# A new price list for a kernel's own scheduler: durations, engine occupation and hand-over delays kept apart

## The chip, the cores and the metric

The kernel runs on one core of one Trainium2 chip. Five engines run their own instruction streams and meet only at semaphores: TensorE (PE, matmuls; its weight loads are listed as PEld), VectorE (DVE), ScalarE (ACT), GpSimd (POOL) and SyncE (SP, which issues the DMAs here). The metric is the device time of one execution, in microseconds; lower is better.

## The reference

Two layers, run twice on one sequence of 2048 tokens of width 448, bf16. Cut to what matters:

```python
def _A_ref(x, mem0, Wq, Wk, Wv, Wo, seg_len):     # 64 segments of 32 tokens, 16 heads of 256
    mem = mem0                                     # 8 memory tokens
    for s in range(n_seg):
        h = concat([mem, x[segment s]])            # 40 tokens
        p = softmax(mask(h Wq (h Wk)^T * scale))
        o = (p (h Wv)) Wo
        mem = o[:, :M]                             # the next segment needs this
        outs.append(o[:, M:])

def _B_ref(x, W_gate, W_up, W_down):
    return (relu(x W_gate) * (x W_up)) W_down

x = x + A(layernorm(x)); x = x + B(layernorm(x))
x = x + A(layernorm(x)); x = x + B(layernorm(x))
```

The memory makes each A layer a recurrence of 64 steps: a segment can't start its scores before the segment ahead has given its 8 memory rows.

## The kernel before

Wq and Wk are multiplied into one matrix A per head at the start, Wv and Wo into one matrix B, so that the scores are h A h^T and the output is p h B. All stays in SBUF after that.

*The recurrence* (`chain`, `middle`). One step serves a segment of both A layers at once, the second layer 7 segments behind. PE multiplies the memory rows by A (L750, eight small tiles at a time), ACT or DVE evicts the four banks to `Usb`, DVE transposes blocks of 32 (L858, L866), PE makes the scores (L881), DVE finds the row minimum (L892), ACT takes the exponentials (L894), DVE normalizes (L898, L899), PE transposes (L914), ACT or DVE evicts, PE applies the probabilities to the rows (L938, L942), an eviction to `YTm`, PE multiplies by B (L785, 56 matmuls in three groups), ACT and DVE split the result in a high and a low part (L792, L793), PE turns it into columns and rows of the next memory (L804, L814), an eviction to `mT`, and the next step begins at L750. `ride` lets some masked rows of the second layer go along (L903 to L911).

*The other work* (`tiles`). For each tile of 128 tokens: the attention of its token rows by four groups of heads (`att_group`: L1021, L1046, a softmax on DVE and ACT at L1053 to L1059, L1065, L938, L1093), the layer norm (`norm`: L957 to L972, a scaled copy `xn`, whose rows a DMA carries to `HR`), and the gated layer (`glu_units`, `glu_down`: L1115, L1120, L1121, L1133). Buffers bound how far this work may run ahead: eight PSUM banks, two `Ug`, one `YT`, one `hG`, two `xn`, six `X`.

*The order* comes from the kernel's own planner. Every operation is recorded by `_Sched.add` with its engine or choice of engines (an eviction may go to ACT or DVE), a cost in ns, what it reads and writes, and a priority (recurrence first). `schedule` then plays the program through: it takes the engine that can start next, and on it, of the operations that are ready at that time, recurrence first, then those in PE's present tiling mode, then program order. The result is a fixed order for each engine, and the choice of ACT or DVE and of the PSUM bank. `emit` writes the order with semaphore waits. Nothing is decided at run time, so an engine whose next instruction isn't ready waits, whatever else could run.

In the planner before, an operation holds its engine for its whole cost. A turn of PE's tiling mode adds 100 ns. A result of PE can be used by another engine 260 ns after its end, any other result 100 ns after, on the same engine 40 ns after. A DMA takes SP for 570 ns and lands 2000 ns after its bytes at 240 bytes per ns. Eviction and matmul costs come from `ev_cost`, `dv_cost` and `mm_cost`; some small operations have a number of their own at the call. In the opening steps, when PE has a gap, `filler` puts dummy matmuls into it (L1148).

Of the kernel before, what the change touches and what calls it, by code (L numbers as in the profile page):

```python
# [31 lines left out]
class _Op:  # L32
    __slots__ = ("idx", "engs", "cost", "fn", "deps", "prio", "dma", "eng", "ndep", "users", "ready",
                 "start", "end", "need_inc", "val", "clock", "slot", "seq", "alloc", "mode",
                 "touch")
# [16 lines left out]
class _Sched:  # L52
# [8 lines left out]
    TURN = 100.0  # L61
# [11 lines left out]
    def add(self, engs, cost, fn, r=(), w=(), prio=1, dma=0, alloc=(), room=(), mode=0, now=None):  # L73
# [4 lines left out]
        o.fn = fn  # L78
        o.deps = {}
# [48 lines left out]

    def schedule(self):
# [33 lines left out]
        while left:  # L163
# [28 lines left out]
            c = o.cost[e]  # L192
            if e == "pe" and self.warm and self.warm[1] <= o.prio[0]:
                bank = self.warm[0]
                if o.prio[0] >= self.warm[2]:
                    if held is not None:
                        empty[bank] = held
                    self.warm = None
                elif held is None and o.prio[1] == 0 and empty[bank][0] is not None:
                    held, empty[bank] = empty[bank], (None, ())  # L200
                n = int((t0 - free[e] - 300.0) * self.warm[3] / 190.0) if self.warm and held else 0
                if n > 0:
                    f = self.filler(n, held[1], free[e], len(seq))
                    order[e].append(f)
                    seq.append(f)
                    mode = f.mode
            if e == "pe":
                if mode is not None and o.mode != mode:
                    c += self.TURN
                mode = o.mode  # L210
            o.start = t0
            if o.dma:
                free[e] = t0 + c
                dma_free = max(dma_free, t0) + o.dma / 240.0
                o.end = dma_free + 2000.0
            else:
                free[e] = t0 + c
                o.end = t0 + c
# [4 lines left out]
            for h in o.touch:  # L223
                h.left -= 1
                if not h.left:
                    empty[h.name] = (max(p.end + (0.0 if p.eng == "pe" else 100.0) for p in h.ops), tuple(h.ops))
            for u in o.users:
                u.ndep -= 1
                for x in u.engs:
                    if o.dma:  # L230
                        t = o.end + 100.0
                    elif x == e:
                        t = o.end if (e == "pe" or u.deps[o] is None) else o.end + 40.0
                    elif e == "pe":
                        t = o.end + 260.0
                    else:
                        t = o.end + 100.0
# [9 lines left out]
    def filler(self, n, deps, start, seq):  # L247
# [5 lines left out]
        f.prio, f.start, f.end, f.need_inc, f.seq, f.users, f.alloc = (0, 9), start, start + n * 190.0, False, seq, [], ()  # L253
# [148 lines left out]
class _Kernel:  # L402
# [190 lines left out]
    def dma(self, dst, src, nbytes, r=(), w=(), prio=1):  # L593
        self.s.add("sp", 570, lambda E, e: E.dma_start(dst, src), r=r, w=w, dma=nbytes, prio=prio)  # L594
# [131 lines left out]
    def chain(self, step):  # L726
# [14 lines left out]
        for half in range(2):  # L741
# [11 lines left out]
            s.add("pe", 7 * (D / 2.33 + 3), fn, r=["mTm", "mTr"] + self.A_all, w=ub, alloc=ub, room=[("Usb", 2 * half + v) for v in range(2)], mode=4, **P)  # L753
# [26 lines left out]
        for lo, hi in ((0, 5), (5, 10), (10, 14)):  # L780
# [7 lines left out]
            s.add("pe", (hi - lo) * (D / 2.33 + 3), oo, r=ykeys + self.B_all, w=[bo], alloc=[bo] if lo == 0 else (), mode=1, **P)  # L788
# [3 lines left out]
        s.add("act", 145 + 0.82 * D, lambda E, e: E.activation(hi_[:, mid], bo.ap()[:, 0:D], ACT.Copy), r=[bo], w=["Ohi"], **P)  # L792
# [58 lines left out]
    def turn_u(self, half, P):  # L851
# [4 lines left out]
        for hh in range(2):  # L856
            out = self.uT[:, 0:3, :, 8 * hh + 4 * half:8 * hh + 4 * half + 4, :].rearrange("p k c a t -> p a (k c) t")
            self.s.add("dve", dv_cost(384), lambda E, e, out=out, hh=hh: E.transpose(out, heads[hh]),  # L858
                       r=[("Usb", 2 * half + v) for v in range(2)], w=[f"uT{half}"], **P)

    def turn_tail(self, hh, P):
# [4 lines left out]
        self.s.add("dve", dv_cost(256), lambda E, e: E.transpose(out, src), r=[("Usb", r) for r in range(4)], w=["uT2"], **P)  # L866

    def middle(self, act, m, row, col, P):
# [15 lines left out]
        s.add("pe", 4 * na * 28, sc, r=uk + [q for c, sg, l in act for q in self.ht_keys(l, sg)], w=[bq], alloc=[bq], **P)  # L884
# [6 lines left out]
        if m["mask"] is None:  # L891
            s.add("dve", dv_cost(40 * na), lambda E, e: E.tensor_reduce(mx, S_(), AX.X, ALU.min), r=[bq], w=[k_("mx")], **P)  # L892
            for c, sg, l in act:
                s.add("act", 214, lambda E, e, c=c: E.activation(m["E"][:, c, 0:L], psS()[:, c, 0:L], ACT.Exp, bias=m["st"][:, c:c + 1], scale=-1.0,  # L894
                                                                 accum_out=m["st"][:, 2 + c:3 + c]), r=[bq, k_("mx")], w=[k_(f"E{c}")], **P)
            for c, sg, l in act:
                b = sg % 2
                s.add("dve", 110, lambda E, e, c=c: E.reciprocal(m["st"][:, 4 + c:5 + c], m["st"][:, 2 + c:3 + c]), r=[k_(f"E{c}")], w=[k_(f"rc{c}")], **P)  # L898
                s.add("dve", 134, lambda E, e, c=c, b=b: E.tensor_scalar(Pv[:, b, 0:L], m["E"][:, c, 0:L], m["st"][:, 4 + c:5 + c], None, op0=ALU.mult),  # L899
                      r=[k_(f"E{c}"), k_(f"rc{c}")], w=[k_(f"P{c}")], **P)  # L900
        else:
# [4 lines left out]
            s.add("act", 165 + 33 * na, lambda E, e: E.activation(E_, T_, ACT.Exp, scale=-1.0), r=[k_("Tm")], w=[k_("Em")], **P)  # L906
            s.add("dve", dv_cost(40 * na), lambda E, e: E.tensor_reduce(sm, E_, AX.X, ALU.add), r=[k_("Em")], w=[k_("sm")], **P)
            s.add("dve", 125, lambda E, e: E.reciprocal(rc, sm), r=[k_("sm")], w=[k_("rc")], **P)
            for c, sg, l in act:
                b = sg % 2  # L910
                s.add("dve", 134, lambda E, e, c=c, b=b: E.tensor_scalar(Pv[:, b, 0:L], m["E"][:, c, 0:L], m["st"][:, 4 + c:5 + c], None, op0=ALU.mult),  # L911
# [16 lines left out]
        s.add("pe", 4 * 56, yy, r=[k_("PT")] + [q for c, sg, l in act for q in self.hr_keys(l, sg)], w=yb, alloc=yb, mode=2, **P)  # L928
# [21 lines left out]
    def norm(self, t, dst):  # L950
# [6 lines left out]
        s.add("dve", 566, lambda E, e: E.bn_stats(st[:, 0:6], X[:, :]), r=[xk], w=[("st", i)])  # L957
        s.add("dve", 134, lambda E, e: E.bn_aggr(st[:, 6:8], st[:, 0:6]), r=[("st", i)], w=[("st2", i)])
        s.add("act", 253, lambda E, e: E.activation(st[:, 8:9], st[:, 7:8], ACT.Ln, bias=self.cvec[:, 0:1], scale=1.0),
              r=[("st2", i), "cvec"], w=[("st3", i)])  # L960
        s.add("act", 204, lambda E, e: E.activation(st[:, 9:10], st[:, 8:9], ACT.Exp, scale=-0.5), r=[("st3", i)], w=[("st4", i)])
# [34 lines left out]
    def att_group(self, l, t, g, bo):  # L996
# [52 lines left out]
        s.add("pe", 16 * 28, sc, r=uk + hk, w=[bs], alloc=[bs], room=[k_("Tx")])  # L1049
# [6 lines left out]
        s.add("act", 296, lambda E, e: E.activation(T[:, :, :], T[:, :, :], ACT.Exp, scale=-1.0), w=[k_("Tx")])  # L1056
        s.add("dve", dv_cost(160), lambda E, e: E.tensor_reduce(sm, T[:, :, :], AX.X, ALU.add), r=[k_("Tx")], w=[k_("sm")])
        s.add("dve", 134, lambda E, e: E.reciprocal(rc, sm), r=[k_("sm")], w=[k_("rc")])
# [12 lines left out]
        for p in range(2):  # L1071
# [10 lines left out]
            s.add("pe", 4 * 56 + 4, yy, r=["PTx"] + hk, w=yb, alloc=yb, room=[("YT", yi, p, h) for h in range(2)], mode=2)  # L1082
# [18 lines left out]
    def glu_units(self, t, g, qs, i):  # L1101
        s = self.s
        G, hG = self.G2[g], self.hG[i]
        for q in qs:
# [15 lines left out]
            s.add("act", 145 + 0.82 * N, lambda E, e, dst=dst, z=two[0], N=N: E.activation(dst, z.ap()[:, 0:N], ACT.Relu), r=[two[0]], w=[("hG", i, q)])  # L1120
# [140 lines left out]
```

## Time and profile before

| | |
|---|---|
| median of 3 runs | 1662.86 us (1659.91 to 1664.81) |
| the profiled execution | 1664.92 us |
| its span, first to last instruction | 1662.8 us |
| instructions | 83559 |
| matmuls, and weight loads | 38134 each |
| DVE, ACT instructions | 3378, 2281 |
| granted TensorE clock, mean | 0.994 |
| bytes moved by DMA | 33.03 MB, mean 20 GB/s |

A profile row of the timeline starts with its start and length in us; then engine, line, operation, output and input tiles and their shapes, and in brackets how long the engine stood idle before it and which instruction released it. A row of a group has its total and its mean ns, then the idle time before it. PE rows overlap: a matmul of 128 columns shows 217 ns (L1021) though the next one starts long before it ends. Line numbers are those of the kernel before; in the changed file the same statement stands up to 7 lines further down.

### The profile page before, as it was taken

The numbers are of one execution on the slowest core, as the hardware profiler recorded it, in microseconds if no ns is written. First come the engines' busy times: TensorE is split into PE (matmuls) and PEld (weight loads), VectorE is DVE, ScalarE is ACT, GpSimd is POOL, SyncE is SP. The second block draws the span as 40 slices with busy tenths as digits, with TensorE's granted clock in tenths as the row PEclk, the third lists the DMA queues.
The fourth block names the chain that finished last, engine by engine and source line by source line (L and its number), as shares of the span: only waits on it lengthen the run. The fifth ranks groups of instructions, "written<-read, shape, count | busy, mean of one in ns | idle before, by whom it ended". The sixth has DMA issues, their size and how long they took to land.

```text
span 1662.8 us, 83559 instructions
## 1 busy us (share of the span) xinstructions
PE 1599.4 (96%) x38134; PEld 1123.4 (68%) x38134; DVE 1167.1 (70%) x3378; ACT 842.1 (51%) x2281; POOL 95.3 (6%) x342
## 2 busy tenths in 40 slices
PE   6999898999999999999999999999999999999997
PEld 4646565677676767766766776776867666767775
DVE  6646565777677777777677876786777777777563
ACT  5734344555555555545454554465455546444442
POOL 2000000000000000000000000000000000000000
PEclk9999999999999999999999999999999999999999
DMA  9350000000000000000000000000000000000000
GB/s 229 103 151 15 5 10 7 6 4 7 7 7 4 14 4 15 4 15 4 4 16 12 7 4 14 4 15 4 12 6 13 7 6 13 4 10 4 12 6 7
DMA packets 44976, 33.03 MB, mean 20 GB/s; under 512 B 17984, under 2 KB 43728, under 8 KB 44624
## 3 DMA queue, kind: packets, MB, share of 16 engines
q1 hardware_dynamic: 44624, 27.70, 6.4%
q8 instruction: 299, 4.90, 1.3%
q14 instruction: 53, 0.43, 0.1%
HBM read 21.36 MB, written 1.84 MB: 14 GB/s over the span
## 4 chain that ended last, share of the span: by engine, by line
PE 79%; DVE 11%; issue 4%; ACT 3%; SPq 2%; DMA 1%; POOL 0%; POOLq 0%; DVEq 0%
PE psG L1021 14%; PE psG L1093 12%; PE psC L785 10%; PE psG L1115 8%; PE psC L750 7%; PE psG L1133 3%; PE psG L750 3%; PE psG L632 3%; DVE uT L858 2%; PE psG L938 2%; SPq L594 2%; PE psG L1046 2%; PE psG L785 2%; PE psC L804 1%; PE psC L814 1%
## 5 line engine op out<-in xcount | busy, mean ns | idle before, releaser
L1093 PE MATMUL psG<-Bsb,YT 128*128 128x448 bf16 x1288 | 273.6, 352 | 3.6 <-DVE YT L349 1.8
L1021 PE MATMUL psG<-HT,A 64*128 64x128 bf16 x5196 | 270.2, 217 | 2.3 <-DVE Usb L349 0.8
L1021 PE MATMUL psG<-HX,A 64*128 64x128 bf16 x3897 | 231.6, 217 | 0.1
L346 ACT ACTIVATE Ug<-psG 64x128 bf16<-64x128 f32 (+2 forms) x454 | 159.4, 375 | 101.8 <-PE psG L1021 91.8
L1115 PE MATMUL psG<-G,glu 64*128 64x128 bf16 x6160 | 188.8, 217 | 3.3 <-DVE G L349 2.2
L1021 PEld LDWEIGHTS psG<-HT,A 64*128 64x128 bf16 x5196 | 181.9, 95 | 13.0 <-issue 4.5
L1115 PEld LDWEIGHTS psG<-G,glu 64*128 64x128 bf16 x6160 | 178.0, 95 | 14.2 <-issue 6.9
L785 PE MATMUL psC<-Bsb,YTm 128*32 128x448 bf16 x3360 | 173.1, 358 | 5.9 <-DVE YTm L349 4.0
L1093 PEld LDWEIGHTS psG<-Bsb,YT 128*128 128x128 bf16 x1288 | 115.2, 98 | 93.5 <-DVE YT L349 2.4
L750 PE MATMUL psG<-A,mT 64*32 64x448 bf16 x4088 | 163.3, 350 | 1.7 <-DVE mT L349 0.9
L858 DVE STREAM_TRANSPOSE uT<-Usb 128x384 bf16<-128x384 bf16 x280 | 156.0, 560 | 4.7 <-ACT Usb L346 0.2
L750 PE MATMUL psC<-A,mT 64*32 64x448 bf16 x3752 | 155.1, 350 | 0.8 <-ACT YT L346 0.4
L1021 PEld LDWEIGHTS psG<-HX,A 64*128 64x128 bf16 x3897 | 147.5, 95 | 0.2 <-issue 0.2
L349 DVE CAST Ug<-psG 64x128 bf16<-64x128 f32 (+2 forms) x287 | 118.3, 428 | 38.5 <-PE psG L1021 34.6
L785 PEld LDWEIGHTS psC<-Bsb,YTm 128*32 128x32 bf16 x3360 | 85.4, 98 | 77.5 <-DVE YTm L349 5.4
L1121 DVE TENSOR_TENSOR hG<-hG,psG 128x512 bf16<-128x512 bf16 (+1 forms) x125 | 75.4, 617 | 66.0 <-ACT hG L1120 65.4
L1120 ACT ACTIVATE hG<-psG 128x512 bf16<-128x512 f32 (+1 forms) x127 | 68.9, 542 | 103.9 <-PE psG L1115 100.4
L346 ACT ACTIVATE YT<-psG 128x448 bf16<-128x448 f32 x222 | 110.5, 548 | 20.9 <-PE psG L942 20.1
L750 PEld LDWEIGHTS psC<-A,mT 64*32 64x32 bf16 x3752 | 80.4, 92 | 59.5 <-DVE PTx L349 2.6
L349 DVE CAST Usb<-psG 128x448 bf16<-128x448 f32 x105 | 63.7, 606 | 60.6 <-PE psG L750 60.4
L346 ACT ACTIVATE Usb<-psC 128x448 bf16<-128x448 f32 x105 | 57.1, 544 | 85.9 <-PE psG L750 65.7
L750 PEld LDWEIGHTS psG<-A,mT 64*32 64x32 bf16 x4088 | 84.2, 92 | 22.3 <-DVE HT L349 4.4
(224 smaller groups left out, 2877.3 us busy)
## 6 DMA issues: line engine op xcount, KB each, us to landing
glu<-in_A_Wo_dram SPq DMA_DIRECT2D x8, 448.0 KB
Bsb<-in_A_Wq_dram SPq DMA_DIRECT2D x8, 384.0 KB
Bsb<-in_A_Wk_dram SPq DMA_DIRECT2D x8, 384.0 KB
glu<-in_A_Wv_dram SPq DMA_DIRECT2D x8, 384.0 KB
HR<-xn SPq DMA_DIRECT2D x128, 24.0 KB
HR<-xn SPq DMA_DIRECT2D x128, 4.0 KB
X<-in_A_x_dram SPq DMA_DIRECT2D x16, 112.0 KB
Tsb<-stage SPq DMA_DIRECT2D x112, 7.0 KB
```

Source lines behind the costliest of these rows:

```text
L346: return E.activation(out, i, ACT.Copy, scale=1.0 if scale is None else scale)
L349: return E.tensor_copy(out, i)
L632: i = E.matmul(bk.ap()[row0:row0 + mn, 0:D], lhsT=lhs[:, et, m0:m0 + mn], rhs=rhs[:, et, :], start=(et == 0), stop=(et == 1), tile_positio ...
L750: i = E.matmul(ub[v].ap()[32 * j:32 * j + 32, 0:D], lhsT=self.mT[rw, b, :], rhs=cols, start=(b == 0), stop=(b == 6), tile_position=(64 * v ...
L785: x = E.matmul(bo.ap()[32 * j:32 * j + 32, 0:D], lhsT=self.YTm[:, q, :], rhs=self.Bsb[:, chunks[q], :], start=(i == 0), stop=(i == 13), ti ...
L858: self.s.add("dve", dv_cost(384), lambda E, e, out=out, hh=hh: E.transpose(out, heads[hh]), r=[("Usb", 2 * half + v) for v in range(2)], w ...
L1021: i = E.matmul(ub[v].ap()[:, 128 * n:128 * n + 128], lhsT=self.A[rw, b, a0:a0 + 128], rhs=HT[rw, b, :, 0:SEG] if b < 4 else HX[rw, b - 4, ...
L1093: i = E.matmul(bo.ap()[:, 0:D], lhsT=YT[:, c, :], rhs=self.Bsb[:, 14 * g + c, :], start=(g == 0 and c == 0), stop=(g == 3 and c == 13))
L1115: i_ = E.matmul(two[v].ap()[:, 128 * c:128 * c + 128], lhsT=self.Wgu[rw, b, f0:f0 + 128], rhs=G[rw, b, :], start=(b == 0), stop=(b == 6), ...
L1120: s.add("act", 145 + 0.82 * N, lambda E, e, dst=dst, z=two[0], N=N: E.activation(dst, z.ap()[:, 0:N], ACT.Relu), r=[two[0]], w=[("hG", i, q)])
L1121: s.add("dve", dv_cost(N), lambda E, e, z=two[1], N=N, dst=dst: E.tensor_tensor(dst, dst, z.ap()[:, 0:N], ALU.mult), r=[two[1]], w=[("hG", ...
L1133: i_ = E.matmul(bk.ap()[:, 0:D], lhsT=hG[:, c, :], rhs=self.Wd[:, c, :], start=(c == 0), stop=(c == NFC - 1))
```

## The change

Only the planner and the costs handed to it change. No instruction is added, removed or altered; which engine evicts a bank, which bank is used, the order on each engine and the number of dummy matmuls follow from the planner.

- An operation on ACT, DVE or POOL now has a duration (until its result is there) and a shorter occupation of its engine: duration less `PIPE` (103, 82 and 60 ns), or `busy` where it is given.
- PE is free when the last matmul has been fed in; the result is there 162 ns later (`PE_END`). A turn (94 ns) delays the start.
- A result reaches another engine after that engine's `SEEN` (58 to PE, 38 to ACT and DVE, 62 to POOL, 60 to SP), the same engine after `SELF` (24, 34, 61).
- A DMA takes SP for 700 ns and lands after 1800 ns.
- The formulas and single costs are replaced: evictions, DVE operations and small ACT operations are longer, matmuls a little shorter.

```diff
-    TURN = 100.0
+    TURN = 94.0
+    PIPE = {"act": 103.0, "dve": 82.0, "pool": 60.0}
+    SELF = {"act": 24.0, "dve": 34.0, "pool": 61.0}
+    SEEN = {"pe": 58.0, "act": 38.0, "dve": 38.0, "pool": 62.0, "sp": 60.0}
+    PE_END = 162.0
...
                 if mode is not None and o.mode != mode:
-                    c += self.TURN
+                    turn = self.TURN
...
-                o.end = dma_free + 2000.0
+                o.end = dma_free + 1800.0
+            elif e == "pe":
+                t0 = max(t0, free[e] + turn)
+                o.start = t0
+                free[e] = t0 + c
+                o.end = t0 + c + self.PE_END
             else:
-                free[e] = t0 + c
+                free[e] = t0 + (c - self.PIPE[e] if o.busy is None else o.busy)
                 o.end = t0 + c
...
-                    empty[h.name] = (max(p.end + (0.0 if p.eng == "pe" else 100.0) for p in h.ops), tuple(h.ops))
+                    empty[h.name] = (max(p.end + (0.0 if p.eng == "pe" else self.SEEN["pe"]) for p in h.ops), tuple(h.ops))
...
-                    if o.dma:
-                        t = o.end + 100.0
-                    elif x == e:
-                        t = o.end if (e == "pe" or u.deps[o] is None) else o.end + 40.0
-                    elif e == "pe":
-                        t = o.end + 260.0
+                    if x == e:
+                        t = o.start if (e == "pe" or u.deps[o] is None) else o.end + self.SELF.get(e, 0.0)
                     else:
-                        t = o.end + 100.0
+                        t = o.end + self.SEEN[x]
...
-    return {"act": 145 + 0.82 * n, "dve": 110 + (0.51 if fast else 1.01) * n}
+    return {"act": 170 + 0.833 * n, "dve": 149 + (0.53 if fast else 1.04) * n, "pool": 170 + 1.0 * n}
...
-    return 106 + (0.51 if fast else 1.01) * n
+    return 149 + (0.53 if fast else 1.04) * n
...
-    return sum(max(n, 62) / 2.33 + 2.6 for n in ns)
+    return sum(max(n, 54) / 2.4 + 2.5 for n in ns)
...
-        self.s.add("sp", 570, lambda E, e: E.dma_start(dst, src), r=r, w=w, dma=nbytes, prio=prio)
+        self.s.add("sp", 700, lambda E, e: E.dma_start(dst, src), r=r, w=w, dma=nbytes, prio=prio)
...
-                s.add("act", 214, lambda E, e, c=c: E.activation(m["E"][:, c, 0:L], psS()[:, c, 0:L], ACT.Exp, bias=m["st"][:, c:c + 1], scale=-1.0,
-                                                                 accum_out=m["st"][:, 2 + c:3 + c]), r=[bq, k_("mx")], w=[k_(f"E{c}")], **P)
+                s.add("act", 382, lambda E, e, c=c: E.activation(m["E"][:, c, 0:L], psS()[:, c, 0:L], ACT.Exp, bias=m["st"][:, c:c + 1], scale=-1.0,
+                                                                 accum_out=m["st"][:, 2 + c:3 + c]), r=[bq, k_("mx")], w=[k_(f"E{c}")], busy=284, **P)
             for c, sg, l in act:
                 b = sg % 2
-                s.add("dve", 110, lambda E, e, c=c: E.reciprocal(m["st"][:, 4 + c:5 + c], m["st"][:, 2 + c:3 + c]), r=[k_(f"E{c}")], w=[k_(f"rc{c}")], **P)
-                s.add("dve", 134, lambda E, e, c=c, b=b: E.tensor_scalar(Pv[:, b, 0:L], m["E"][:, c, 0:L], m["st"][:, 4 + c:5 + c], None, op0=ALU.mult),
+                s.add("dve", 156, lambda E, e, c=c: E.reciprocal(m["st"][:, 4 + c:5 + c], m["st"][:, 2 + c:3 + c]), r=[k_(f"E{c}")], w=[k_(f"rc{c}")], **P)
+                s.add("dve", 238, lambda E, e, c=c, b=b: E.tensor_scalar(Pv[:, b, 0:L], m["E"][:, c, 0:L], m["st"][:, 4 + c:5 + c], None, op0=ALU.mult),
                       r=[k_(f"E{c}"), k_(f"rc{c}")], w=[k_(f"P{c}")], **P)
```

More of the change, by code (lines that the diff above doesn't have):

```diff
@@ L34 @@
                  "start", "end", "need_inc", "val", "clock", "slot", "seq", "alloc", "mode",
-                 "touch")
+                 "touch", "busy")
 class _Bank:
@@ L71, in __init__, with add @@
         self.alias = {}
-    def add(self, engs, cost, fn, r=(), w=(), prio=1, dma=0, alloc=(), room=(), mode=0, now=None):
+    def add(self, engs, cost, fn, r=(), w=(), prio=1, dma=0, alloc=(), room=(), mode=0, now=None, busy=None):
         o = _Op()
@@ L78, in add @@
         o.fn = fn
+        o.busy = busy
         o.deps = {}
@@ L192, in schedule @@
             c = o.cost[e]
+            turn = 0.0
             if e == "pe" and self.warm and self.warm[1] <= o.prio[0]:
@@ L252, in filler @@
         f.deps = {d: True for d in deps}
-        f.prio, f.start, f.end, f.need_inc, f.seq, f.users, f.alloc = (0, 9), start, start + n * 190.0, False, seq, [], ()
+        f.prio, f.start, f.end, f.need_inc, f.seq, f.users, f.alloc, f.busy = (0, 9), start, start + n * 190.0, False, seq, [], (), None
         return f
@@ L752, in fn @@
                 return i
-            s.add("pe", 7 * (D / 2.33 + 3), fn, r=["mTm", "mTr"] + self.A_all, w=ub, alloc=ub, room=[("Usb", 2 * half + v) for v in range(2)], mode=4, **P)
+            s.add("pe", mm_cost(*[D] * 7), fn, r=["mTm", "mTr"] + self.A_all, w=ub, alloc=ub, room=[("Usb", 2 * half + v) for v in range(2)], mode=4, **P)
             for v in range(2):
@@ L787, in oo @@
                 return x
-            s.add("pe", (hi - lo) * (D / 2.33 + 3), oo, r=ykeys + self.B_all, w=[bo], alloc=[bo] if lo == 0 else (), mode=1, **P)
+            s.add("pe", mm_cost(*[D] * (hi - lo)), oo, r=ykeys + self.B_all, w=[bo], alloc=[bo] if lo == 0 else (), mode=1, **P)
         hi_, lo_ = self.Ohi, self.Olo
         mid = slice(64, 64 + D)
-        s.add("act", 145 + 0.82 * D, lambda E, e: E.activation(hi_[:, mid], bo.ap()[:, 0:D], ACT.Copy), r=[bo], w=["Ohi"], **P)
+        s.add("act", 170 + 0.833 * D, lambda E, e: E.activation(hi_[:, mid], bo.ap()[:, 0:D], ACT.Copy), r=[bo], w=["Ohi"], **P)
         s.add("dve", dv_cost(D), lambda E, e: E.tensor_tensor(lo_[:, mid], bo.ap()[:, 0:D], hi_[:, mid], ALU.subtract),
@@ L857, in turn_u @@
             out = self.uT[:, 0:3, :, 8 * hh + 4 * half:8 * hh + 4 * half + 4, :].rearrange("p k c a t -> p a (k c) t")
-            self.s.add("dve", dv_cost(384), lambda E, e, out=out, hh=hh: E.transpose(out, heads[hh]),
+            self.s.add("dve", 578, lambda E, e, out=out, hh=hh: E.transpose(out, heads[hh]),
                        r=[("Usb", 2 * half + v) for v in range(2)], w=[f"uT{half}"], **P)
@@ L865, in turn_tail @@
         out = self.uT[rows, 3, :, 8 * hh:8 * hh + 8, :].rearrange("p c a t -> p a c t")
-        self.s.add("dve", dv_cost(256), lambda E, e: E.transpose(out, src), r=[("Usb", r) for r in range(4)], w=["uT2"], **P)
+        self.s.add("dve", 420, lambda E, e: E.transpose(out, src), r=[("Usb", r) for r in range(4)], w=["uT2"], **P)
     def middle(self, act, m, row, col, P):
@@ L883, in middle @@
         uk = ["uT0", "uT1", "uT2"]
-        s.add("pe", 4 * na * 28, sc, r=uk + [q for c, sg, l in act for q in self.ht_keys(l, sg)], w=[bq], alloc=[bq], **P)
+        s.add("pe", mm_cost(*[L] * (4 * na)), sc, r=uk + [q for c, sg, l in act for q in self.ht_keys(l, sg)], w=[bq], alloc=[bq], **P)
         S_ = lambda: psS()[:, c0:c1, 0:L]
@@ L927, in yy @@
             return i
-        s.add("pe", 4 * 56, yy, r=[k_("PT")] + [q for c, sg, l in act for q in self.hr_keys(l, sg)], w=yb, alloc=yb, mode=2, **P)
+        s.add("pe", mm_cost(*[128] * 3, 64, 64), yy, r=[k_("PT")] + [q for c, sg, l in act for q in self.hr_keys(l, sg)], w=yb, alloc=yb, mode=2, **P)
         for (c, _, _), bk in zip(act, yb):
@@ L1048, in att_group @@
         hk = list(dict.fromkeys(k for q in range(4) for k in self.ht_keys(l, 4 * t + q)))
-        s.add("pe", 16 * 28, sc, r=uk + hk, w=[bs], alloc=[bs], room=[k_("Tx")])
+        s.add("pe", mm_cost(*[L] * 16), sc, r=uk + hk, w=[bs], alloc=[bs], room=[k_("Tx")])
         mk = self.maskb[:, :].unsqueeze(1).to_broadcast([128, 4, L])
@@ L1081, in att_group @@
             hk = [q for h in range(2) for q in self.hr_keys(l, 4 * t + 2 * p + h)]
-            s.add("pe", 4 * 56 + 4, yy, r=["PTx"] + hk, w=yb, alloc=yb, room=[("YT", yi, p, h) for h in range(2)], mode=2)
+            s.add("pe", mm_cost(*[128] * 3, 64, 64), yy, r=["PTx"] + hk, w=yb, alloc=yb, room=[("YT", yi, p, h) for h in range(2)], mode=2)
             for h in range(2):
@@ L1119, in glu_units @@
             dst = hG[:, 4 * q:4 * q + n, :].rearrange("p a b -> p (a b)")
-            s.add("act", 145 + 0.82 * N, lambda E, e, dst=dst, z=two[0], N=N: E.activation(dst, z.ap()[:, 0:N], ACT.Relu), r=[two[0]], w=[("hG", i, q)])
+            s.add("act", 170 + 0.833 * N, lambda E, e, dst=dst, z=two[0], N=N: E.activation(dst, z.ap()[:, 0:N], ACT.Relu), r=[two[0]], w=[("hG", i, q)])
             s.add("dve", dv_cost(N), lambda E, e, z=two[1], N=N, dst=dst: E.tensor_tensor(dst, dst, z.ap()[:, 0:N], ALU.mult),
```

18 lines of the change are left out of this document (9 added, 9 removed).

## The prediction

> **What bounds the kernel.** I read the busy table first, then the span in stretches, then the chain, then the waits.
>
> ```profile
> PE 1599.4 (96%) x38134; PEld 1123.4 (68%) x38134; DVE 1167.1 (70%) x3378; ACT 842.1 (51%) x2281; POOL 95.3 (6%) x342
> ...
> PE 79%; DVE 11%; issue 4%; ACT 3%; SPq 2%; DMA 1%; POOL 0%; POOLq 0%; DVEq 0%
> ```
>
> TensorE (PE) is the bound: busy for 1599.4 of 1662.8 us, and 79% of the chain that ended last. No instruction changes, so the time can move only through PE's idle time and what a different order of matmuls costs. The stretches (columns: window, its length, then busy time and count for PE, PEld, DVE, ACT, POOL, then clock and DMA) show where the idle 63.4 us lies:
>
> ```profile
> 0.00:104.00 104.00, 91.09 (x1102) 56.70 (x1106) 66.49 (x138) 62.42 (x106) 9.63 (x29) 1.00 0.58 155
> 104.00:304.00 200.00, 179.26 (x4260) 117.78 (x4264) 117.83 (x323) 83.72 (x236) 8.70 (x30) 0.98 0.12 28
> 304.00:700.00 396.00, 388.42 (x9660) 273.79 (x9654) 295.92 (x893) 211.60 (x602) 24.53 (x91) 1.00 0.03 8
> 700.00:1100.00 400.00, 393.25 (x9793) 282.13 (x9790) 296.99 (x892) 209.66 (x592) 23.20 (x86) 1.00 0.04 9
> 1100.00:1500.00 400.00, 394.19 (x9795) 280.29 (x9784) 296.96 (x893) 208.13 (x580) 24.38 (x89) 1.00 0.03 8
> 1500.00:1602.00 102.00, 101.57 (x2447) 72.57 (x2444) 66.84 (x179) 46.85 (x122) 4.61 (x16) 1.00 0.03 7
> 1602.00:1662.80 60.80, 51.59 (x1115) 40.17 (x1109) 26.07 (x63) 19.73 (x47) 0.30 (x1) 0.94 0.03 8
> ```
>
> Weights and first step: 12.9 us idle. The first steps of the recurrence, before the tile work piles up: 20.7. The steady part, 304 to 1602 us: 7.6 + 6.8 + 5.8 + 0.4 = 20.6. The tail: 9.2. The first two and the last are mostly short of work: a new order has nothing to put there. The steady part is where planning can matter.
>
> **Part 1: tile-mode turns (added).** PE pays when it changes its tiling. In time order, with the group of L1133:
>
> ```profile
> 399.78 0.92 PE L1093 MATMUL psG<-Bsb,YT 128*128 128x448 bf16 x4
> 400.63 0.34 PE L938 MATMUL psC<-PTm,HR 40*128 40x128 bf16 x6
> ...
> 405.68 1.12 PE L1093 MATMUL psG<-Bsb,YT 128*128 128x448 bf16 x5
> 406.64 0.17 PE L804 MATMUL psC<-Sel,Ohi 128*128 128x16 bf16 x1
> ...
> 1657.02 2.82 PE L1133 MATMUL psG<-glu,hG 128*128 128x448 bf16 x14
> L1133 PE MATMUL psG<-glu,hG 128*128 128x448 bf16 x392 | 86.1, 353 | 0.1
> ```
>
> A 448-column matmul follows the last one after (2.82 - 0.35) / 13 = 0.190 us. So the four at 399.78 are fed in by 400.54, and the row-tiled L938 starts 0.09 late; the five at 405.68 are fed in by 406.63, and L804, untiled too, starts 0.01 later. A turn costs 0.093 us (the middle of the 678 boundaries of this kind in the trace). Counted in the two built orders, turns go from 678 to 697: 19 x 0.093 = +1.8 us. Bounds: 0 where a turn falls into a wait, 1.8 otherwise; I take 1.8, since most turns follow work directly. The Trainium skill's page TensorEngine Tiling (Array Packing), Tiling Modes, says that changing the mode drains TensorE; a whole tail, taken as 0.353 - 0.190 = 0.16 us, would make this +3.1 instead of +1.8, and the trace's 0.09 decides against that.
>
> **Part 2: the chain's links (moved).** The recurrence (priority 0) is planned with new durations. Groups by form, one softmax in time order, and what PE's weight loads waited for there (us, times, longest):
>
> ```profile
> L346 ACT ACTIVATE YT<-psG 128x448 bf16<-128x448 f32 x222 | 110.5, 548 | 20.9 <-PE psG L942 20.1 <-PE psC L942 0.5
> L349 DVE CAST YT<-psG 128x448 bf16<-128x448 f32 x153 | 90.6, 616 | 11.3 <-PE psG L942 10.9
> L894 ACT ACTIVATE Tm<-psC,stm 128x40 f32<-128x40 f32 x108 | 30.8, 290 | 31.1 <-DVE stm L892 30.6
> L894 ACT ACTIVATION_READ_ACCUMULATOR Tm<-psC,stm 128x1 f32 x108 | 21.3, 197 | 0.0
> L899 DVE TENSOR_SCALAR Pm<-Tm,stm 128x40 bf16<-128x40 f32 x126 | 27.4, 239 | 1.0
> ...
> 701.61 0.57 PE L881 MATMUL psC<-HT,uT 128*128 128x40 bf16 x16
> 702.05 0.23 DVE L892 TENSOR_REDUCE stm<-psC 128x2 f32<-128x80 f32 x1
> 702.78 0.20 ACT L894 ACTIVATION_READ_ACCUMULATOR Tm<-psC,stm 128x1 f32 x1
> 703.16 0.40 DVE L899 TENSOR_SCALAR Pm<-Tm,stm 128x40 bf16<-128x40 f32 x2
> 704.23 0.13 PEld L914 LDWEIGHTS psC<-ident,Pm 128*104 128x104 bf16 x1
> ...
> PEld psC L914 <- DVE Pm L899: 11.0, 20, 1.6
> ```
>
> The old planner takes 214 ns for an exponential (L894) that shows 290 and then 197 for its sum, and 134 for L899 that shows 239. From PE's end at L881 to the next matmul L914 it plans 260 + 187 + 100 + 428 + 100 + 284 + 100 = 1.46 us. In the rows, the chain's 8 of the 16 matmuls are in by 701.80, and the second L899 ends at 703.56, plus 0.06 to reach PE: 1.81 us. The new figures (200 + 232 + 38 + 284 + 382 + 38 + 156 + 34 + 238 + 58) give 1.66. Evictions err the other way: the old plan has 260 + 512 + 100 for a 448-column one on ACT where 200 + 548 + 58 is nearer.
>
> What that does to PE can be counted. I laid both orders end to end at the trace's own pitches and turns, and measured the PE work standing between the two ends of each link, 70 steps, against the link's latency in the trace. Steps from the 12th on (58), shortfall summed, before to after: L881 to L914 (1.81) 2.5 to 0; L914 to L938 (0.54) 1.6 to 0.8; L938 to L785 (0.85) 2.3 to 0.7; L785 to L804 (1.47) 0.6 to 0.9; L750 to L881 (3.18, the DVE transposes) 0.6 to 1.2; L804 to the next L750 (0.66) 0 to 0.1. Sum 7.6 to 3.7: -3.9 us. The first 12 steps: 16.3 to 19.8, +3.5. There the count says less: with little tile work, an early and a late place leave the same gap on PE. Bounds -3 to +3.5; I take +1, as the cover lost is largely cover by work that then stands elsewhere.
>
> **Part 3: the DMAs behind VectorE (moved).** Waits, and the place in time order:
>
> ```profile
> DVE xn L963 <- DMA HR<-xn: 12.2, 9, 3.1
> ...
> 1007.53 7.40 SPq L594 DMA_DIRECT2D HR<-xn  x8
> 1016.17 0.40 DVE L963 TENSOR_SCALAR xn<-X,lnst 128x448 bf16<-128x448 bf16 x1 [3.15 <-DMA HR<-xn]
> 1016.98 0.56 PE L972 MATMUL psG<-ident,xn 128*128 128x128 bf16 x7 [1.90 <-POOL xn L966]
> ```
>
> VectorE works in order. It stood 3.15 us for eight transfers out of the buffer it was to overwrite; the softmax of the chain stood behind it, and PE lost 1.90 us. The old plan gives eight issues 8 x 570 + 2000 = 6.6 us, the new one 8 x 700 + 1800 = 7.4; the rows show 8.6 from the first issue to the release. The error falls from 2.0 to 1.2 us. All nine such waits sum to 12.2 us; PE feels a part. Bounds 0 to -4 (two thirds of the largest shows on PE, and several are hidden); I take -2.
>
> **Part 4: ACT and DVE (moved).** Counted in the orders, 428 evictions go from DVE to ACT and 354 back, 74 net: 74 x 0.616 = 46 us less on DVE, 74 x 0.548 = 41 us more on ACT. Both have room (1167 and 842 of 1663 us). PE waits that a DVE queue causes may shorten. Bounds -4 to 0, I take -2. Against this stand the covers of other PE work, shortened because the new plan trusts its shorter hand-over times: of 200 L1021 groups those with under 0.86 us since the producer of what they need go from 16 to 33, of 140 L750 groups those under 0.70 from 8 to 14; tile groups L938, L1093, L1065 and L972 gain. Laid out the same way with the quarter-point of each latency, all waits come to 52 us before and 55 after. That is the main unknown: -4 to +10; I take 0, the sum of links that gain and links that lose.
>
> **Part 5: the clock.** Windows again:
>
> ```profile
> 1019.00:1022.40 3.40, 3.33 (x62) 2.92 (x62) 1.63 (x4) 1.17 (x3) 0.00 (x0) 0.51 0.25 72
> 1343.40:1346.80 3.40, 3.40 (x40) 1.53 (x36) 0.40 (x1) 0.39 (x2) 0.30 (x1) 0.50 0.02 5
> ```
>
> Right after clustered waits the granted clock was half for 3.4 us, up to 1.7 us lost each. Two such windows lie in the steady part. If one goes: -1.3; bounds -3.4 to +3.4 (two more). The Trainium skill, TensorE: Matmul & The Clock Gate, The HAM clock gate, ties half clock to a whole idle window of about 3.4 us; no PE wait here is that long before 1019 us (1.90 the longest shown), so the measurement decides that shorter gaps are enough. By the page waits this short could not bring such a window, and the term would be 0 instead of -1.3.
>
> Dummy matmuls (L1148) go from 78 to 77: nothing; they fill waits. SP issues the same DMAs, POOL the same copies.
>
> **Sum.** +1.8 - 3.9 + 1 - 2 - 2 + 0 - 1.3 = -6.4 us on the profiled execution's own 1664.92 us (span 1662.8 and 2.1 around it): 1658.5. The median of the runs shown, 1662.86, is 2.1 below that execution, so 1656.4; I say 1656. No change means within 0.3%, 5 us, about what a measurement of this kernel can tell.
>
> **The rivals.**
> 1. *Nothing changes.* The waits of the steady part only move: -3.9 in the links is paid back by turns (+1.8) and thinner tile covers (+2): 1662.8, and 1658 to 1668 as a band. For it: 52 against 55 us. Against: the links that gain are those where the old figures are plainly wrong.
> 2. *Slower: thin covers.* PE comes to L1021 and L750 before the evictions that free their banks and bring their input. Place: the eviction rows above (548, 616 ns) on engines already in the middle of another half-microsecond instruction, which delays a hand-over by 0.3 us on average. With each link's middle latency instead of its quarter-point my layout has 83 us of waits before and 93 after: +10.6, with the turns +12.4: 1675. It decides if real latencies stay at the present middle, that is, if better planned queues don't shorten them.
> 3. *Faster than forecast.* Both bounds of parts 3 and 4 come in: 1.8 - 3.9 - 3 - 4 - 4 - 4 - 3.4 = -20.5: 1642.
>
> **Chances.** Forecast and rival 3 together (over 5 us faster) 0.44: the main mis-planned links are repaired, and they lie in 80% of the span. Rival 1: 0.24. Rival 2: 0.32, since shorter hand-over times remove margin everywhere and the layout speaks for it. The range goes from rival 3's 1640 to 1677, just past rival 2; the likeliest case alone spans 1648 to 1658.
>
> **What would show it.** Turns: more boundaries between row-tiled and untiled groups, same 0.09. Links: the PEld waits at L914 on DVE Pm (11.0 us in 20) at half or less; L804 waits on Olo unchanged. DMAs: DVE waits on HR<-xn at 6 us or less. Engines: DVE busy near 1121, ACT near 883. Steady stretch: PE idle 14 us or less in place of 20.6. Wrong if that idle is 20 or more, if waits before L1021 or L750 rise by several us, or if half-clock windows appear in the steady part.

## The result

The changed kernel takes 1652.93 us (median of 4 runs, 1648.65 to 1653.65) against 1662.49 (median of 4, 1659.91 to 1664.81): a ratio of 0.9938, 95% interval 0.9915 to 0.996. The forecast was 1656. Its profiled execution took 1652.99 us with a span of 1651.1. Of the page after, the busy table and the chain by engine:

```profile
PE 1593.8 (97%) x38133; PEld 1121.1 (68%) x38133; DVE 1139.8 (69%) x3304; ACT 865.8 (52%) x2355; POOL 94.9 (6%) x342
...
PE 85%; DVE 7%; issue 3%; ACT 3%; DMA 1%; SPq 1%; POOL 0%; POOLq 0%; DVEq 0%
```

The chain that ended last runs through PE for 85% in place of 79%, and through DVE for 7% in place of 11%. (ACT's 2355 instructions are 127 more than the 2228 operations placed there, 2154 before: the reads of the exponentials' sums and a table load.) The stretches after, columns as before:

```profile
0.00:104.00 104.00, 90.17 (x1097) 56.64 (x1097) 66.47 (x137) 60.85 (x105) 9.54 (x29) 1.00 0.57 155
104.00:304.00 200.00, 180.75 (x4282) 118.29 (x4284) 117.64 (x325) 86.42 (x241) 8.73 (x30) 0.97 0.12 28
304.00:700.00 396.00, 390.55 (x9763) 276.12 (x9756) 292.38 (x889) 218.95 (x621) 24.48 (x91) 1.00 0.03 8
700.00:1100.00 400.00, 394.82 (x9783) 282.21 (x9781) 285.99 (x859) 215.48 (x609) 23.79 (x88) 1.00 0.04 9
1100.00:1500.00 400.00, 395.65 (x9866) 282.92 (x9863) 292.48 (x879) 220.98 (x626) 24.01 (x89) 1.00 0.03 8
1500.00:1590.00 90.00, 89.89 (x2298) 65.72 (x2300) 57.29 (x152) 43.53 (x109) 3.13 (x11) 1.00 0.03 8
1590.00:1651.00 61.00, 52.01 (x1071) 39.25 (x1059) 27.56 (x68) 19.60 (x47) 1.19 (x4) 0.94 0.03 8
```

Start, early steps and tail are as they were: idle 13.8, 19.3 and 9.0 us against 12.9, 20.7 and 9.2. In the steady part PE's idle time fell from 20.6 to 5.5 + 5.2 + 4.4 + 0.1 = 15.1 us. That is only half of the gain, because a PE row outlasts its feeding by some 0.16 us and hides the start of each wait. Laid against the pitch of its own groups, PE's time between two groups that is neither feeding nor a turn says more (an estimate from the traces' rows): 36.5 us before and 22.3 after in the steady part, -14.2; start and early steps 43.3 and 42.7, tail 9.3 and 9.0. The turns rose by 1.7 us. Nearly all of the gain lies in the steady part.

Waits over 0.05 us in the steady part, outside stretches of half clock, went from 131 with 36.3 us to 102 with 26.1. By the group that waited (lines of before):

| group | before, us (count) | after |
|---|---|---|
| L938, chain and tiles | 6.4 (22) | 2.5 (15) |
| L785 | 5.5 (15) | 2.3 (9) |
| L914 | 4.6 (20) | 0.7 (4) |
| L972 | 4.1 (6) | 1.3 (4) |
| L881 | 2.5 (10) | 2.0 (5) |
| L750 | 2.7 (9) | 3.6 (11) |
| L804 | 0.9 (1) | 1.5 (2) |
| L1021 | 3.9 (21) | 9.1 (30) |

The clock adds to this: the two half-clock stretches of the steady part, which held 2.3 us of lost time, have no counterpart between 267 and 1635 us after. Waits (-10.2), clock (-2.3), start and tail (-0.9) and turns (+1.7) sum to the 11.7 us by which the span fell. The -14.2 counted by pitch is 1.7 more than waits and clock; these estimates are good to some 2 us. Of the waits after, over the whole span, those that the prediction named (us, times, longest):

```profile
PEld psC L921 <- DVE Pm L906: 8.7, 19, 1.8
PEld psC L811 <- DVE Olo L800: 7.0, 9, 1.7
PE psC L1028 <- ACT YT L353: 2.3, 7, 0.5
PE psG L757 <- ACT mT L353: 1.8, 4, 0.4
DVE xn L970 <- DMA HR<-xn: 4.5, 5, 1.9
```

Before, the first of them was 11.0 us in 20 and the second this:

```profile
PEld psC L804 <- DVE Olo L793: 5.9, 12, 1.2
```

So the wait at L914 fell in the steady part (4.6 to 0.7 us in the table), but over the whole span only by 2.3 us.

### The profile page after: what moved, and what is told of

It reads as the page before. It is cut to its first block, busy times and chain, and to the rows that moved or that the text cites. A ratio compares the mean times of both kernels' runs of the same rounds, so it can differ in the third digit from the quotient of the medians.

```text
span 1651.1 us, 83525 instructions
## 1 busy us (share of the span) xinstructions
PE 1593.8 (97%) x38133; PEld 1121.1 (68%) x38133; DVE 1139.8 (69%) x3304; ACT 865.8 (52%) x2355; POOL 94.9 (6%) x342
## 4 chain that ended last, share of the span: by engine, by line
PE 85%; DVE 7%; issue 3%; ACT 3%; DMA 1%; SPq 1%; POOL 0%; POOLq 0%; DVEq 0%
PE psG L1028 14%; PE psG L1100 14%; PE psC L792 10%; PE psG L1122 10%; PE psC L757 8%; PE psG L1140 4%; PE psG L639 3%; PE psG L757 2%; PE psG L1053 2%; PE psG L945 2%; PE psG L792 2%; PE psC L821 2%; DVE uT L865 1%; PE psC L811 1%; PE psC L945 1%
## 5 line engine op out<-in xcount | busy, mean ns | idle before, releaser
L1100 PE MATMUL psG<-Bsb,YT 128*128 128x448 bf16 x1400 | 297.8, 352 | 2.2 <-ACT YT L353 1.2
L1028 PE MATMUL psG<-HT,A 64*128 64x128 bf16 x5196 | 269.5, 216 | 3.3 <-DVE YT L356 1.8
L1028 PE MATMUL psG<-HX,A 64*128 64x128 bf16 x3897 | 231.9, 216 | 0.1
L1100 PEld LDWEIGHTS psG<-Bsb,YT 128*128 128x128 bf16 x1400 | 126.6, 98 | 98.2 <-ACT YT L353 2.1
L1028 PEld LDWEIGHTS psG<-HT,A 64*128 64x128 bf16 x5196 | 181.8, 94 | 10.7 <-ACT YT L353 2.4
L1122 PE MATMUL psG<-G,glu 64*128 64x128 bf16 x5936 | 180.4, 217 | 1.0 <-ACT G L353 1.0
L1122 PEld LDWEIGHTS psG<-G,glu 64*128 64x128 bf16 x5936 | 169.1, 95 | 10.6 <-issue 7.5
L792 PE MATMUL psC<-Bsb,YTm 128*32 128x448 bf16 x3192 | 165.2, 359 | 2.9 <-DVE YTm L356 1.5
L757 PE MATMUL psC<-A,mT 64*32 64x448 bf16 x3892 | 166.9, 350 | 0.9 <-DVE mT L356 0.4
L1028 PEld LDWEIGHTS psG<-HX,A 64*128 64x128 bf16 x3897 | 147.6, 94 | 0.3 <-issue 0.3
L757 PEld LDWEIGHTS psC<-A,mT 64*32 64x32 bf16 x3892 | 86.2, 92 | 67.4 <-DVE HT L356 7.0
L353 ACT ACTIVATE Usb<-psC 128x448 bf16<-128x448 f32 x120 | 64.3, 544 | 87.6 <-PE psG L757 67.6
L356 DVE CAST YTm<-psC 128x448 bf16<-128x448 f32 x79 | 49.2, 622 | 83.8 <-PE psG L949 53.0
L356 DVE CAST YT<-psG 128x448 bf16<-128x448 f32 x154 | 92.4, 616 | 13.8 <-PE psG L949 10.6
```

Of the source, the lines that this page charges most:

```text
L353: return E.activation(out, i, ACT.Copy, scale=1.0 if scale is None else scale)
L356: return E.tensor_copy(out, i)
L757: i = E.matmul(ub[v].ap()[32 * j:32 * j + 32, 0:D], lhsT=self.mT[rw, b, :], rhs=cols, start=(b == 0), stop=(b == 6), tile_position=(64 * v ...
L792: x = E.matmul(bo.ap()[32 * j:32 * j + 32, 0:D], lhsT=self.YTm[:, q, :], rhs=self.Bsb[:, chunks[q], :], start=(i == 0), stop=(i == 13), ti ...
L1028: i = E.matmul(ub[v].ap()[:, 128 * n:128 * n + 128], lhsT=self.A[rw, b, a0:a0 + 128], rhs=HT[rw, b, :, 0:SEG] if b < 4 else HX[rw, b - 4, ...
L1100: i = E.matmul(bo.ap()[:, 0:D], lhsT=YT[:, c, :], rhs=self.Bsb[:, 14 * g + c, :], start=(g == 0 and c == 0), stop=(g == 3 and c == 13))
```

## The experiments

Three theories stood against each other: A, a price list without bias gives the gain; B, one half of the list (the costs, or the way in which engines are held and results handed over) gives it alone; C, a greedy planner's order is redrawn by any change, and this draw was lucky. PE's busy time between 304 and 1500 us (1196 us) is used throughout as a short view of the steady part:

Before, and then the changed kernel:

```profile
304.00:1500.00 1196.00, 1175.86 (x29233) 836.20 (x29226) 889.87 (x2677) 629.39 (x1773) 72.11 (x266) 1.00 0.03 8
```

```profile
304.00:1500.00 1196.00, 1181.02 (x29405) 841.25 (x29398) 870.85 (x2623) 655.42 (x1855) 72.29 (x268) 1.00 0.04 8
```

PE is idle for 20.1 us of it before and for 15.0 after.

**The two halves.** The first takes the costs of the change with the planner of before, the second the planner of the change with the costs of before.

```diff
 # e1_costs_only: class _Sched as before; ev_cost, dv_cost, mm_cost and all costs at the calls as changed
 # e2_delays_only: class _Sched as changed; ev_cost, dv_cost, mm_cost and all costs at the calls as before
```

> The planner of the kernel before (an operation holds its engine for its whole cost, 260 and 100 ns between engines, 40 on the same one, a DMA lands after 2000) with the new costs of the operations. 701 turns, 2220 evictions and other operations on ACT. Theory A (the gain is the mis-planned durations, the softmax above all): ratio to before 0.992 to 0.997, and PEld waits at the transpose after the softmax fall as in the changed kernel. Theory B (the gain is occupation and delays): 1.00, or over it, since longer costs that hold the engine whole make ACT and DVE look slower than they are. Theory C (the gain is what any redrawn order may bring by chance): anywhere from 0.990 to 1.005, without relation to e2.

> The other half: the planner of the changed kernel (occupation, measured delays, 1800 ns for a DMA) with the costs of the kernel before (570 for a DMA issue among them). 664 turns, 14 fewer than before. Theory A: 0.999 to 1.006, since the costs are now too short and the delays no longer make up for it. Theory B: 0.992 to 0.997. Theory C: anywhere from 0.990 to 1.005.

Measured: the costs alone 1.0038 (1.002 to 1.0057), the planner alone 1.0506 (1.0487 to 1.0524). Neither half gives a gain; B falls, and A in the form in which the durations carry it alone. The second run lies far outside all three ranges expected. Its steady part:

```profile
304.00:1500.00 1196.00, 1120.45 (x27217) 784.01 (x27224) 831.62 (x2489) 596.66 (x1670) 66.66 (x247) 0.99 0.03 8
```

75.6 us of idle PE, in waits everywhere (the longest sums from 304 to 1590 us):

```profile
PE psG L979 <- POOL xn L973: 9.7, 10, 2.6
PE psC L888 <- DVE uT L873: 7.3, 14, 1.2
PE psC L921 <- DVE Pm L906: 7.3, 12, 1.5
PE psC L921 <- DVE Pr L918: 7.2, 15, 0.9
PE psG L1122 <- DVE hG L1128: 6.9, 7, 3.4
```

**Single parts of the change taken back.** The DMA figures, and the softmax durations of the recurrence:

```diff
 # e3_dma_old, from the changed kernel
-        self.s.add("sp", 700, lambda E, e: E.dma_start(dst, src), r=r, w=w, dma=nbytes, prio=prio)
+        self.s.add("sp", 570, lambda E, e: E.dma_start(dst, src), r=r, w=w, dma=nbytes, prio=prio)
-                o.end = dma_free + 1800.0
+                o.end = dma_free + 2000.0
 # e4_softmax_old, from the changed kernel: L894 as 214, L898 as 110, L899 (and its twin
 # behind the masked rows' exponential) as 134, each of them held whole
```

> The changed kernel with the DMA figures of before (570 for an issue, 2000 to land). If the DMA figures carry part of the gain, as the prediction's part 3 has it (2 us), DVE's waits for the transfers out of xn rise again towards 12 us and the ratio to before is 0.995; if they carry nothing, 0.994 as the changed kernel, with those waits unchanged from it.

> The changed kernel with the three durations of the recurrence's softmax as before (214 for the exponential, 110 and 134 for what follows). The prediction's part 2 puts 2.5 us of the gain into this link in the steady part. Then waits of PE before the transpose after the softmax come back to some 10 us in all and the ratio to before is 0.996 or more. If the link was covered anyway, 0.994.

Measured: 0.9942 (0.9921 to 0.9964) and 0.9928 (0.9912 to 0.9945), both the changed kernel's ratio. With the old DMA figures DVE still waits only this much for the transfers out of `xn`:

```profile
DVE xn L970 <- DMA HR<-xn: 4.7, 5, 1.3
```

So that wait fell, but not through the DMA figures. With the old softmax the wait that they were to repair does come back:

```profile
PEld psC L921 <- DVE Pm L906: 12.4, 30, 1.7
```

In the steady part the waits at this group are 4.6 us again (0.7 in the changed kernel), as before the change. But those at the tile groups L1028 are 3.4 instead of 9.1, and the sums are nearly equal, 28.8 and 26.1 us. Here, what one link gave back, another took.

**Luck.** One number moved by 2 ns in each kernel:

```diff
 # n1_pe_end_164, from the changed kernel
-    PE_END = 162.0
+    PE_END = 164.0
 # n3_before_262, from the kernel before
-                        t = o.end + 260.0
+                        t = o.end + 262.0
```

> The changed kernel with one number 2 ns off (PE_END 164 for 162), which redraws the order (703 turns in place of 697). Theory A (the gain comes from a price list without bias): within 0.3% of the changed kernel, 0.991 to 0.997 of before. Theory C (the luck of a greedy order): may lie anywhere from 0.988 to 1.005.

> The kernel before with one number 2 ns off (262 for 260 from PE to the others; 680 turns for 678). Theory A: within 0.3% of before. Theory C: may lie anywhere from 0.990 to 1.010; if it reaches 0.994, the change's gain is no more than a redraw brings.

Measured: 0.9935 (0.9914 to 0.9956) and 0.9988 (0.9975 to 1.0001). Each stays with its parent, and the two pairs stay 0.5% apart: a redraw as small as this is worth 0.1%, and C in its simple form falls.

**Occupation, and a late plan.**

```diff
 # e5_hold_whole, from the changed kernel
-    PIPE = {"act": 103.0, "dve": 82.0, "pool": 60.0}
+    PIPE = {"act": 0.0, "dve": 0.0, "pool": 0.0}
 # (the exponential of L894 keeps its own occupation, 284 of 382)
 # e6_seen_plus60, from the changed kernel
-    SEEN = {"pe": 58.0, "act": 38.0, "dve": 38.0, "pool": 62.0, "sp": 60.0}
+    SEEN = {"pe": 118.0, "act": 98.0, "dve": 98.0, "pool": 122.0, "sp": 120.0}
```

> The changed kernel with occupation equal to the duration (PIPE 0), all else new: ACT, DVE and POOL look 60 to 103 ns slower per instruction than they are. If keeping occupation apart carries the gain: 0.998 to 1.004 of before. If the costs with the short delays carry it: 0.992 to 0.996.

> The changed kernel with 60 ns more on each hand-over between engines: a plan that is late by a known amount. If thin covers cost (the prediction's rival 2), this gains: 0.988 to 0.992 of before, with fewer waits at L757 and L1028. If a plan without bias is best and lateness costs little, 0.994 to 0.998.

Measured: 1.0035 (1.002 to 1.005) without separate occupation, 0.9963 (0.9946 to 0.998) with 60 ns more on every hand-over. Given the new costs and delays, taking occupation back loses the whole gain and 0.35% besides. The late plan does have fewer waits before L1028, 3.9 us against 9.1, and is no faster. One reason is the granted clock: 0.991 to 0.993 over its six executions, 0.993 to 0.997 over the changed kernel's four.

**The other corners.** With costs (C), occupation (O) and delays (D) each old or new there are eight kernels; five are above, the kernel before and the change among them. Three more:

```diff
 # f110_costs_occupation, from the changed kernel: delays as before, 40 on the same engine,
 # 260 from PE (162 + 98), 100 between others
 # f010_occupation: the same planner with the costs of before
 # f001_delays: the planner of the change with PIPE 0, with the costs of before
```

> New costs and new occupation with the delays of before (260 ns from PE, 100 between others, 40 on the same engine). Theory A1 (occupation kept apart, on true durations, is the whole gain; long delays cost little, as the run with 60 ns more says): 0.994 to 0.998 of before. Theory A2 (the measured delays carry a part of their own): 0.999 to 1.004.

> Old costs and old delays with the new occupation alone: the planner then believes that DVE is free 82 ns and ACT 103 ns before the old costs end, which for short operations is far earlier than it is. Theory O (a plan that takes an engine for faster than it is makes everything behind it late; this is what made costs of before with occupation and delays of now 5% slower): 1.02 to 1.05. Theory D (that loss came from the short delays): 0.995 to 1.005.

> Old costs, held whole, with the new delays alone. Theory O: 0.998 to 1.01. Theory D: 1.02 to 1.05.

The planner's other new figures (the turn ahead of the start, 1800 ns for a DMA) come with O and with D, the 700 ns of a DMA issue with C. The last column is an estimate: the same ratio with each execution's time multiplied by its granted clock, that is, as if the half-clock stretches had cost nothing.

| new | ratio to before (95%) | PE idle, 304 to 1500 us | at full clock |
|---|---|---|---|
| none (before) | 1 | 20.1 | 1 |
| C | 1.0038 (1.002 to 1.0057) | 20.9 | 0.999 |
| O | 1.0299 (1.0268 to 1.033) | 47.4 | 1.027 |
| D | 1.0103 (1.0079 to 1.0127) | 30.3 | 1.008 |
| C, O | 1.0061 (1.0038 to 1.0085) | 26.0 | 0.998 |
| C, D | 1.0035 (1.002 to 1.005) | 21.3 | 0.998 |
| O, D | 1.0506 (1.0487 to 1.0524) | 75.6 | 1.044 |
| C, O, D (the change) | 0.9938 (0.9915 to 0.996) | 15.0 | 0.993 |

As they ran, any one or two of the parts lose, and all three together win. The ranges expected for the costs with occupation (0.994 to 0.998, and 0.999 to 1.004) were both missed on the slow side, and the delays alone end just above the 1.01 of theory O. That occupation without the new costs is harmful, 1.0299, holds.

The three small losses (C; C, O; C, D), however, lie in the clock. The time lost to half clock, time multiplied by one less the granted clock, is in the mean 14.0 us with C, 15.4 with C and D and 18.8 with C and O, against 5.8 to 6.6 for the kernel before in the same series and 8.7 for the change. At full clock these three would stand 0.1 to 0.2% ahead of before. (For the change, whose own series has no clocks of before on record, the 41 later executions of before stand in.) So it is shown that no part and no pair of them gave the gain in these runs, but not that C, alone or in a pair, makes the waits longer than before.

Why O without C is so costly may be read from rows of before:

```profile
712.92 1.15 DVE L349 CAST YTm<-psG 128x448 bf16<-128x448 f32 x2
```

Two evictions of 0.62 us take 1.15 us, so one holds DVE for 0.53. The plan before holds it for 562 ns, the changed one for 615 - 82 = 533, old costs with occupation for 480, new costs without it for 615. A plan that takes DVE for a tenth faster than it is would make every queue behind it late; one that takes it for slower would only miss chances. The prices fit this reading, +3% for O and +5% for O with D on the one side, +0.4% for C and for C with D on the other, and +1% for D with the old, short costs; but no run changes the figure of these evictions alone.

The costs with occupation and old delays differ from the run with 60 ns more on each hand-over by at most 24 ns between engines and 40 ns on the same one, yet they stand 1% apart. The reason is in PE's waits of the first:

```profile
PE psG L923 <- DVE Pm L908: 10.2, 6, 1.8
PE psC L890 <- DVE uT L875: 5.8, 5, 1.2
```

and in the places, of which three read:

```profile
793.95 0.57 PE L890 MATMUL psC<-HT,uT 128*128 128x40 bf16 x16 [1.16 <-DVE uT L875]
796.20 0.26 PE L923 MATMUL psG<-ident,Pm 128*104 128x128 bf16 x1 [1.69 <-DVE Pm L908]
978.89 0.57 PE L890 MATMUL psC<-HT,uT 128*128 128x40 bf16 x16 [1.16 <-DVE uT L875]
981.15 0.26 PE L923 MATMUL psG<-ident,Pm 128*104 128x128 bf16 x1 [1.69 <-DVE Pm L908]
1163.76 0.57 PE L890 MATMUL psC<-HT,uT 128*128 128x40 bf16 x16 [1.16 <-DVE uT L875]
1166.02 0.26 PE L923 MATMUL psG<-ident,Pm 128*104 128x128 bf16 x1 [1.69 <-DVE Pm L908]
```

The same two waits come every 185 us: the work repeats itself every eight steps, the planner answers the same situation the same way, and one bad place costs a multiple. A half-clock stretch follows at all six places, which adds to the 16 us of waits. So theory C keeps a part: not a redraw of 2 ns, but one of some 20 ns can bring or remove such a place, worth 1%. With that, what D adds to C and O stays open: without this one place the pair might stand near the change.

**The choice of engine.**

```diff
 # e7_engines_before, from the changed kernel; CHOICE has the engine of each of the evictions in the kernel before
         o.engs = (engs,) if isinstance(engs, str) else tuple(engs)
+        if len(o.engs) > 1:
+            o.engs = (("act", "dve")[int(CHOICE[self.n_two])],)
+            self.n_two += 1
```

> The changed kernel's planner, but each eviction is held to the engine it had in the kernel before (2154 operations on ACT, 3378 on DVE, 703 turns); only order and banks are new. If the 74 operations that moved from DVE to ACT carry 2 us or more, as the prediction's part 4 has it: 0.995 to 1.002 of before. If the choice of engine doesn't matter: 0.994.

Measured: 1.0033 (1.0018 to 1.0049), slower than both ranges. All of the gain is gone (at full clock too, 1.001), the steady waits are 38.6 us, and DVE again waits for the transfers out of `xn`:

```profile
DVE xn L983 <- DMA HR<-xn: 8.7, 7, 2.8
```

The choice of engine is not a side effect. The run doesn't tell whether the 74 operations moved matter, or that each eviction goes to the engine that is really free first: holding the planner to any fixed list takes both away.

## Why the prediction was right, point by point

- *Turns.* Predicted +1.8 us; 678 and 697 at 0.093 gave +1.7, and a turn costs the same in the trace after (0.092 to 0.095 us). Right.
- *The links.* Predicted -3.9 in the steady part, -2.5 of it at L914, -1.6 at L785, -0.8 at L938. The waits there fell by 3.9, 3.2 and 3.9 (the last with the tiles' share). Right in place and low in size. The sign that was asked for, weight loads waiting half as long at L914 over the whole span, did not come (11.0 to 8.7 us), and those at L804 rose from 5.9 to 7.0 instead of staying. But the reason given, that the softmax durations are repaired, is not what the kernel's time rests on: with the old durations the waits at L914 return and the time stays at 0.9928. The step failed in taking a repaired link for a gain; in a plan this full its cover is taken from another group.
- *The first steps.* Predicted +1, within -3 to +3.5; waits up to 304 us went from 43.3 to 42.7. The reading that this stretch lacks work and not planning was right.
- *The DMAs.* Predicted -2, by the new DMA figures. DVE's waits on them fell from 12.2 to 4.5 us (6 or less was asked) and those of L972 by 2.8, but with the old figures they are 4.7. The size was right, the cause wrong; the run with the old engine choice, 8.7, points at the order and choice on DVE.
- *ACT and DVE.* Predicted -2 from the shift. DVE's busy time fell by 27 us, not 46, and ACT's rose by 24, not 41, probably because an operation moved was counted by its whole row where rows overlap (0.53 held of 0.62), and because the 782 exchanged ones differ in size. As a cause this step was the most undersized: with the old choice nothing is gained.
- *The clock.* Predicted -1.3 for one half-clock stretch less; in the profiled pair both of the steady part went, worth 2.3. That is the luck of this pair: the granted clock of before ranged from 0.994 (the profiled execution) to 0.998 over its later executions, and the changed kernel loses more to half clock (8.7 us in the mean) than before in its later series (5.8 to 6.6).
- *Thin covers (rival 2).* Its mechanism is there: waits before L1021 rose from 3.9 to 9.1 us and before L750 from 2.7 to 3.6. It was named as the way to be slower, and several us more before L1021 as a sign of being wrong; that sign came. The forecast put the term at 0, and it took 6 us of a larger gain instead. The rival's price rested on latencies staying at their present middle; whether they shortened was not measured.
- *Sum.* Predicted -6.4, measured -11.9 on the profiled executions (1664.92 and 1652.99) and -9.6 on the medians. What the parts lack is the steady part's -12.5 to -14.2, of which the terms there held about -9 with the clock (-3.9 - 2 - 2 - 1.3). The place of the gain and its sign were foreseen; that the number came within 4 us is in part luck, since links too small and thin covers put at 0 offset each other.

## What to carry to other kernels

A planner's prices work together: here an engine held too long, hand-overs set too long and durations set too short seem to have made up for each other, and correcting one or two of them gave no gain and up to 5% of loss. Between two wrong prices the one that makes an engine look slow was the cheaper here: 0.4 to 1% against 3 to 5%. And before a local repair is counted as a gain, ask whose cover it uses; where the bound engine is 97% busy, test the list as a whole, and look for the one wait that returns with the period of the work. Before a difference under 1% is put down to the plan, set the granted clock of both sides beside it.

## What the runs showed of the hardware

The granted clock halves without a whole stretch of idle PE. In the run with costs, occupation and old delays, stretches of 3.4 us with little PE work, and the stretches right after them:

```profile
794.59:798.00 3.41, 1.25 (x23) 0.93 (x27) 3.34 (x17) 2.38 (x10) 0.29 (x1) 1.00 0.00 0
1163.30:1166.70 3.40, 0.88 (x19) 0.65 (x21) 3.30 (x15) 1.66 (x8) 0.29 (x1) 0.99 0.00 0
...
798.00:801.40 3.40, 3.40 (x40) 1.64 (x44) 0.05 (x1) 0.68 (x1) 0.00 (x0) 0.50 0.00 0
1166.70:1170.10 3.40, 3.40 (x42) 2.09 (x46) 1.25 (x4) 1.46 (x2) 0.00 (x0) 0.51 0.01 2
```

And in the kernel before, ahead of its two half-clock stretches of 1019.0 and 1343.4 us, with the stretch before the first of them:

```profile
1012.00:1015.60 3.60, 3.08 (x32) 1.68 (x27) 1.02 (x2) 1.36 (x3) 0.46 (x2) 1.00 0.09 20
1015.60:1019.00 3.40, 1.89 (x31) 1.22 (x31) 2.25 (x8) 2.08 (x7) 0.30 (x1) 1.00 0.02 3
1340.00:1343.40 3.40, 2.17 (x31) 1.12 (x32) 3.11 (x12) 1.54 (x6) 0.00 (x0) 0.99 0.00 0
```

PE busy for 2.17 of 3.40 us, its rows' tails included, was little enough; 3.08 of 3.60 was not followed by a slow stretch. So waits of 1 to 2 us cost more when they fall together: the next 3.4 us then run at half speed.

The 14 traces together tell where the limit lies. In each, the half-clock stretches that begin within the span start whole multiples of 3.413 us apart (to 3 ns) and last one or two of these lengths. Cut into windows on this grid, from 104 us on, they hold 6298 windows at full clock. All 45 in which PE rows cover less than 1.6 us of the 3.41 were followed by a half-clock stretch, none of the 6168 with more than 2.18 us was, and of the 85 between 26 were. Where the grid lies differs from trace to trace, so whether two waits fall into one window or into two would be in part chance; this may be why the granted clock of one kernel differs between executions.
